# Attention times V in a fused transformer block: the third and fourth block of a chunk next to each other

## The chip, the cores and the metric

The kernel runs on one core of a Trainium2 chip. The metric is device time in microseconds (us). PE stands for TensorE (matmuls), PEld for its weight loads, DVE for VectorE, ACT for ScalarE, POOL for GpSimd and SP for SyncE, which here only issues DMAs.

## What is computed

S = 2048 rows of D = 576, H = 32 heads of 18, a hidden width F = 4608, and a causal window of 256 keys, all in bf16:

```
xn = layernorm(x)
q, k, v = split(xn @ wqkv)                       # 32 heads, Dh = 18
p = softmax(where(0 <= i - j < 256, q @ k.T * Dh**-0.5, -1e9))
h = silu(xn @ w1) * (xn @ w3)
out = x + (p @ v) @ wo + h @ w2
```

## The kernel before

The rows are taken in four chunks of 512 (`c` = 0 to 3). A chunk has three stretches on the PE, and the PE's order is written out by hand: the program lists every operation once, in one order, and each engine does its own share of the list in that order. Waits are worked out from the buffers that an operation reads and writes (`_Prog.resolve`).

- **Projections** (`proj_part`, L490): q, k and v of the chunk. q and k go through `stage` and are repacked into `qv` and `kv` by DMAs on SP and ACT (`span_main`, `span_last`, L555).
- **First half of the MLP, the units** (`unit_pairs`, L726): 36 units, each of 128 hidden features; a unit is nine pairs of matmuls of 512 columns, on two tiles of 64 rows by 128 columns of the PE. A unit takes one of three pairs of PSUM banks in turn (`job`). Then `unit_tanh` (ACT, L735) and `unit_h` (DVE, L741 and L744) make `hT[u]`. Between the pairs stand the **score steps**: `scores` (PE, L610) into a fixed pair of banks, `exps` (ACT, L619) into a slot, `masks` (POOL, L646). A chunk has 32 (chunk 0) or 40 score steps, eight groups `g` of four heads.
- **Second half of the MLP** (`p2_list`, `p2_item`, L797): the sum over 36 tiles of `hT` times w2, for each half of the output's columns (half 0, then half 1); at the end of each half the output projection `wo` of the attention's result `oT`, the residual (L828) and the output DMA. 16 items, 32 matmuls of 288 columns, make a w2 tile's worth. In half 0 the first rows of `wo` need the packs of blocks 0 to 2, and its later rows those of block 3.

**Attention times V** is done in four blocks a chunk (`pv(c, j, banks)`, L667), block j for the groups 2j and 2j + 1. A block is 72 (chunk 0) or 96 matmuls on eight tiles of 64 rows by 32 columns, of which 20 columns are used. After a block come `pv_out` (DVE transposes of two PSUM banks, L676), `o_scale` (a DVE reciprocal, L681, and a POOL product, L682), `o_turn` (DVE transposes, L689) and `o_pack` (four DMAs on SP, L714) into `oT`. Blocks 0, 1 and 2 stand between units, each when its scores are at least `PV_AFTER` = 20 matmul pairs old by the planner's `clock`; each takes a bank pair from `job` and counts `PV_COST` = 6.6 pairs, and the score steps are spread over what remains. Block 3 stands in the second half after item 8, in the banks of unit 34.

**Slots.** The result of a score step lies in a slot until its block has read it: ten buffers `pt`, four pairs of `stage` tiles (chunks 1 to 3), and for the first four steps of a chunk the last eight tiles of `hT`, which the units write later.

**Weights.** w1 and w3 come in nine tiles a chunk, each in six DMAs on SP (`load_part`, L320), into three buffers `w13`. Behind units 3, 7, ... up to 27 six parts are owed, issued one by one behind pairs of the next units; six more are issued in the second half at items 170 to 295, each behind a PE instruction. The tiles of w2 (`load_w2`, L352, ACT's queue, some on SP) are asked for six tiles ahead; in the second half four of their eight buffers lie in `w13[1]`. On SP also stand, in program order, the transposing DMA of the next chunk's last rows (L446, item 40), loads of x (items 100 and 120) and the swapped copy of xn for the next chunk (L453, item 300).

Of the kernel before, what the change touches and what calls it, by code (L numbers as in the profile page):

```python
# [5 lines left out]
dt = mybir.dt  # L6
ACT = mybir.ActivationFunctionType
ALU = mybir.AluOpType
# [156 lines left out]
def bass_parallel_sum__sliding_block__glu_gated_swiglu__prompt_kernel(  # L165
# [32 lines left out]
    with ExitStack() as es:  # L198
# [3 lines left out]

        NXP, NOF, NPT, NW13, NW2, NOD, AHEAD = 7, 4, 10, 3, 4, 2, 6
        KB, NB, NV = 64, CH // 64, 12
        ident = sb("ident", [128, 128])
        xp = [sb(f"xp{i}", [128, D]) for i in range(NXP)]
        xn = [sb(f"xn{i}", [128, 640]) for i in range(2)]
# [25 lines left out]
        def pt_slot(sl):  # L233
            kind, n = sl
            if kind == "pt":
                return pt[:, n, :, :]
            if kind == "sh":
                two = stage[:, 2 * n:2 * n + 2, :]
            else:
                two = hT[:, NF - 8 + 2 * n:NF - 6 + 2 * n, :]  # L240
            return two.rearrange("p t c -> p (t c)").rearrange("p (q r) -> p q r", r=2)

        def pt_keys(sl):
            kind, n = sl
            if kind == "pt":
                return [("pt", n)]
            if kind == "sh":
                return [("sh", 2 * n), ("sh", 2 * n + 1)]
            return [("h", NF - 8 + 2 * n), ("h", NF - 7 + 2 * n)]

        def st_keys(*tiles):
            return [("sh", t) for t in tiles]

        uq = sb("uq", [128, CH], dt.float32)
        rden = sb("rden", [128, CH // 32], dt.float32)
        oq = sb("oq", [128, CH])
        od = [sb(f"od{i}", [128, 2, CH]) for i in range(NOD)]
        oT = sb("oT", [128, 5, CH])
# [289 lines left out]
        def span_issue(a, b, moves, first, only=slice(None)):  # L548
            seen = set()
            for n, (kind, eng, tset, dst, src) in enumerate(moves):  # L550
                if n not in range(len(moves))[only]:
                    seen.add(kind)
                    continue
                keys = [(kind, g) for g in range(a, b)]
                add(eng, lambda e, dst=dst, src=src: e.dma_start(dst, src), r=st_keys(*tset), dma=f"{kind}_{a}",  # L555
                    **{"j" if kind in seen or not first else "w": keys})
                seen.add(kind)

# [45 lines left out]
        def scores(c, g, s):  # L604
            col = 0
            for n, (kb, q0, nb) in enumerate(steps_of(c)[s]):
# [6 lines left out]
                        r=[("kp" if kb < 0 else "k", g), ("q", g)], **{"j" if n else "w": [("ps", SC[r])]})  # L613
                col += nb

        def exps(c, g, s, sl):
            pt_of[(c, g, s)] = sl
            w = KB * sum(nb for _, _, nb in steps_of(c)[s])
            add("act", lambda e: e.activation(  # L619
                pt_slot(sl)[:, 0:w, :], PS[:, SC[0]:SC[1] + 1, 0:w].rearrange("p r q -> p q r"), ACT.Exp, scale=scale),  # L620
                r=[("ps", b) for b in SC], w=pt_keys(sl))

        def masks(c, g, s):

# [24 lines left out]
        def pv(c, j, banks):  # L649

            seen = set()
            n_all = sum(len(st) for st in steps_of(c))
            n = 0
            for s, st in enumerate(steps_of(c)):
                col = 0
                for kb, q0, nb in st:
                    n += 1
                    pos = (c * NB + kb) % NV
                    for gi in range(2):
                        g = 2 * j + gi  # L660
                        sl = pt_of[(c, g, s)]
                        for pr in range(2):
                            for p in range(2):
                                first = (p, gi, pr) not in seen
                                seen.add((p, gi, pr))
                                q = 2 * gi + pr
                                add("pe", lambda e, p=p, q=q, pr=pr, sl=sl, g=g, pos=pos, q0=q0, nb=nb, col=col, first=first, n=n: e.matmul(  # L667
                                    PS[32 * q:32 * q + VW, banks[p], q0 * KB:(q0 + nb) * KB],
                                    va[64 * p:64 * p + 64, pos, g, pr, :],
                                    pt_slot(sl)[64 * p:64 * p + 64, col * KB:(col + nb) * KB, pr],  # L670
                                    start=first, stop=(n == n_all), tile_position=(64 * p, 32 * q), skip_group_check=True),
                                    r=pt_keys(sl) + [("va", pos)], **{"j" if any(k[0] == p for k in seen - {(p, gi, pr)}) or not first else "w": [("ps", banks[p])]})
                    col += nb

        def pv_out(b, i):
            add("dve", lambda e: e.transpose(uqs[i], PS[:, b, :]), r=[("ps", b)], w=uq_keys[i])  # L676

        def o_scale(i):
            u3 = uqs[i].rearrange("p (n d) -> p n d", d=32)
            o3 = oq[:, :].rearrange("p (n d) -> p n d", d=32)[:, :, 0:Dh]  # L680
            add("dve", lambda e: e.reciprocal(rden[:], u3[:, :, Dh]), r=uq_keys[i], w=["rden"])  # L681
            add("pool", lambda e: e.tensor_tensor(  # L682
                o3, u3[:, :, 0:Dh], rden[:].unsqueeze(2).to_broadcast([128, CH // 32, Dh]), ALU.mult),
                r=uq_keys[i] + ["rden", "oq0"], w=["oq"])

        def o_turn(g, half):
            i = g // 2 % NOD
# [310 lines left out]
        for c in range(NC):  # L998
# [5 lines left out]
            loads = {8: (2,), 17: (3,)} if c + 1 < NC else {}  # L1004
            if c == 0:
                loads = {11: (0,), 13: (1,), 15: (2,), 17: (3,)}
            total = 9 * NF + len(att) + 3 * PV_COST
            if c:
                total += 9 * sum(COST[kind] for kind, _ in PROJ)
            start = 60 if c == 0 else 46  # L1010
# [3 lines left out]
            done = 0  # L1014
            pv_ready = {}
            free = [("pt", n) for n in range(NPT)]
            if c:
                free += [("sh", n) for n in range(4)]
            early = [("h", n) for n in range(4)]
            side = {}  # L1020
            jobs = {}
            next_pv = 0
# [4 lines left out]
            def take(n):  # L1027
                if n < len(early):
                    return early[n]
                return free.pop(0)  # L1030

            def score_step():
                nonlocal done
                g, s = att[done]
                scores(c, g, s)
                sl = take(done)
                exps(c, g, s, sl)
                masks(c, g, s)
                done += 1
                if done % (2 * NS) == 0:  # L1040
                    pv_ready[done // (2 * NS) - 1] = clock + PV_AFTER

            def spaced_step():
                nonlocal nxt, soon, clock
                score_step()
                soon = clock + 7.5
                room = last - clock - PV_COST * (3 - next_pv) - 5 * sum(v > at_u for v in xt)
                nxt = max(soon, clock + room / max(1, len(att) - done))
                clock += 1

# [18 lines left out]
            for u in range(NF):  # L1069
# [13 lines left out]
                    if n in (3, 8):  # L1083
                        owe_part(op)
                unit_tanh(u, b0[0])
                if u % 4 == 3 and u < NF - 8 and (c or u != 15):
                    owed += 6
                if next_pv in pv_ready and clock >= pv_ready[next_pv] and next_pv < 3:
# [5 lines left out]
                    for g in (2 * j, 2 * j + 1):  # L1094
                        for s in range(NS):
                            if pt_of[(c, g, s)][0] != "h":
                                free.append(pt_of[(c, g, s)])
                    later(u, lambda b=banks: (pv_out(b[0], 0), pv_out(b[1], 1), o_scale(0)))
                    later(u + 1, lambda j=j: (o_turn(2 * j, 0), o_turn(2 * j, 1), o_scale(1)))
# [40 lines left out]
            assert done == len(att) and next_pv == 3, (done, next_pv)  # L1140
# [9 lines left out]
            for item in p2_list(c):  # L1150
# [31 lines left out]
        with nc.Block() as block:  # L1182
# [29 lines left out]
```

## Time and profile before

| what | us |
|---|---|
| median of 3 runs (lowest, highest) | 558.04 (557.98, 558.10) |
| span of the profiled execution | 556.1 |
| median less span | 1.94 |
| PE in units (L726), busy, by the four tile groups of the page and its views | 182.3 + 155.3 + 5.4 + 4.7 |
| PE in the second half (L797): w2, wo | 143.9 + 20.5 |
| PE in projections (L490) | 39.0 + 22.1 |
| PE in scores (L610) | 53.8 + 19.8 |
| PE in attention times V (L667): 1068 + 216 + 156 matmuls | 20.5 + 7.8 + 4.3 |
| DVE in one unit (L741, L744), mean of one | 0.681, 0.687 |
| ACT in one exponential (L619), mean of one | 1.010 |
| w1/w3 part, w2 tile: issue to landing, median over the run | 4.3, 3.5 |

The profile is of one execution; for it the profile lists the span, from the first to the last instruction, and the timed runs are beside it with what lies around the span. Busy times of the PE overlap where tiles work side by side, so they don't add up to the span; the chain of waits in order of time gives each line's share without overlap. Starts are measured and the ends of matmuls are modelled, so a loss on the PE is read from starts. An "x4" behind a form counts instructions, and eight tiles working side by side are eight instructions. The page's "idle before" leaves out gaps below 150 ns.

### The profile page before, as it was taken

The numbers are of one execution on the slowest core, as the hardware profiler recorded it, in microseconds if no ns is written. First come the engines' busy times: TensorE is split into PE (matmuls) and PEld (weight loads), VectorE is DVE, ScalarE is ACT, GpSimd is POOL, SyncE is SP. The second block draws the span as 40 slices with busy tenths as digits, with TensorE's granted clock in tenths as the row PEclk, the third lists the DMA queues.
The fourth block names the chain that finished last, engine by engine and source line by source line (L and its number), as shares of the span: only waits on it lengthen the run. The fifth ranks groups of instructions, "written<-read, shape, count | busy, mean of one in ns | idle before, by whom it ended". The sixth has DMA issues, their size and how long they took to land.

```text
span 556.1 us, 18239 instructions
## 1 busy us (share of the span) xinstructions
PE 552.4 (99%) x8022; PEld 348.8 (63%) x8022; DVE 310.8 (56%) x587; ACT 257.6 (46%) x365; POOL 160.0 (29%) x380
## 2 busy tenths in 40 slices
PE   8999999999999999999999999999999999999998
PEld 4555445677687455477767645547777654555776
DVE  7466798610456778851056668884105567767211
ACT  7456776100286767600047776650005676666000
POOL 5323454300034445330003344533000333433000
PEclk9999999999999999999999999999999999999999
DMA  9997899677566556656856746566683684650650
GB/s 255 203 197 161 201 215 182 171 179 191 139 139 149 135 147 151 155 148 176 205 109 137 171 110 170 126 163 164 158 205 83 138 174 124 151 135 21 174 152 22
DMA packets 128038, 86.00 MB, mean 155 GB/s; under 512 B 35702, under 2 KB 125646, under 8 KB 127958
## 3 DMA queue, kind: packets, MB, share of 16 engines
q1 hardware_dynamic: 89138, 62.80, 49.7%
q10 hardware_dynamic: 38820, 22.02, 16.0%
q8 instruction: 63, 1.03, 0.8%
q14 instruction: 17, 0.14, 0.1%
HBM read 71.29 MB, written 2.36 MB: 132 GB/s over the span
## 4 chain that ended last, share of the span: by engine, by line
PE 98%; DMA 1%; ACT 0%; DVE 0%; issue 0%
PE ps L726 51%; PE ps L797 29%; PE ps L490 10%; PE ps L610 6%; PE ps L667 4%; DMA xp<-in_A_x_dram 1%; DVE stats L386 0%; ACT hT L380 0%; PE ps L419 0%; ACT sd L359 0%; ACT xnT L432 0%; DVE ofin L819 0%; DVE mv L389 0%
## 5 line engine op out<-in xcount | busy, mean ns | idle before, releaser
L726 PE MATMUL ps<-xnT,w 64*128 64x512 bf16 x1400 | 182.3, 376 | 0.0
L726 PE MATMUL ps<-xnS,w 64*128 64x512 bf16 x1120 | 155.3, 376 | 0.0
L797 PE MATMUL ps<-w,hT 64*128 64x288 bf16 x2292 | 143.9, 282 | 0.0
L741 DVE SCALAR_TENSOR_TENSOR gs<-th,ps 128x512 bf16<-128x512 bf16 x144 | 98.0, 681 | 80.1 <-ACT th L735 79.1
L619 ACT ACTIVATE pt<-ps 128x1024 bf16<-128x1024 f32 (+1 forms) x112 | 113.2, 1010 | 63.8 <-PE ps L610 62.5
L797 PEld LDWEIGHTS ps<-w,hT 64*128 64x128 bf16 x2292 | 112.0, 94 | 29.4 <-issue 0.4
L726 PEld LDWEIGHTS ps<-xnT,w 64*128 64x128 bf16 x1400 | 73.8, 94 | 55.0
L646 POOL TENSOR_TENSOR pt<-pt,mk 128x128 int32<-128x128 int32 (+1 forms) x199 | 80.3, 426 | 79.5 <-ACT pt L619 79.5
L744 DVE SCALAR_TENSOR_TENSOR hT<-gs,ps 128x512 bf16<-128x512 bf16 x144 | 98.9, 687 | 5.0
L735 ACT ACTIVATE th<-ps 128x512 bf16<-128x512 f32 x144 | 85.4, 593 | 22.2 <-PE ps L726 21.9
L726 PEld LDWEIGHTS ps<-xnS,w 64*128 64x128 bf16 x1120 | 60.1, 94 | 50.1
L503 ACT ACTIVATE stage<-ps 128x512 bf16<-128x512 f32 x16 | 9.6, 597 | 142.8 <-PE ps L490 140.5
L828 DVE TENSOR_TENSOR ofin<-ps,xp 128x288 bf16<-128x288 f32 x31 | 12.2, 451 | 110.3 <-PE ps L797 110.3
L646 POOL TENSOR_TENSOR hT<-hT,mk 128x128 int32<-128x128 int32 (+1 forms) x31 | 12.4, 420 | 170.5 <-ACT hT L619 170.5
L610 PE MATMUL ps<-qv,kv 64*128 64x320 bf16 (+4 forms) x528 | 53.8, 260 | 0.0
L610 PEld LDWEIGHTS ps<-qv,kv 64*128 64x128 bf16 x528 | 28.5, 94 | 24.7 <-issue 0.3
L490 PE MATMUL ps<-xnT,wp 64*128 64x512 bf16 (+1 forms) x360 | 39.0, 355 | 0.0
L619 ACT ACTIVATE stage<-ps 128x1024 bf16<-128x1024 f32 x24 | 24.6, 1024 | 12.6 <-PE ps L610 12.6
L689 DVE STREAM_TRANSPOSE od<-oq 128x256 bf16<-128x256 bf16 x64 | 25.8, 428 | 6.3 <-POOL oq L682 6.3
L490 PEld LDWEIGHTS ps<-xnT,wp 64*128 64x128 bf16 x360 | 20.6, 94 | 12.6 <-ACT va L539 0.4
L490 PE MATMUL ps<-wv,xnT 64*128 64x288 bf16 x288 | 22.1, 284 | 0.2 <-ACT xnT L432 0.2
L646 POOL TENSOR_TENSOR stage<-stage,mk 128x128 int32<-128x128 int32 (+1 forms) x42 | 16.9, 421 | 17.4 <-ACT stage L619 17.3
(73 smaller groups left out, 337.6 us busy)
## 6 DMA issues: line engine op xcount, KB each, us to landing
w<-in_B_w_dram SPq DMA_DIRECT2D x210, 192.0 KB, 4.3
w<-in_B_w_dram ACTq DMA_DIRECT2D x70, 288.0 KB, 3.5
xp<-in_A_x_dram SPq DMA_DIRECT2D x29, 144.0 KB, 3.3
out_dram<-ofin SPq DMA_DIRECT2D x31, 72.0 KB, 3.2
xnS<-xnT SPq DMA_DIRECT2D x8, 256.0 KB, 5.2
oT<-od SPq DMA_DIRECT2D x56, 36.0 KB
pt<-in_A_wqkv_dram SPq DMA_DIRECT2D x4, 288.0 KB, 5.0
hT<-in_B_w_dram SPq DMA_DIRECT2D x6, 192.0 KB, 6.3
```

What stands on the lines that cost most here:

```text
L490: op = add("pe", lambda e, out_=out_, st=st, mv=mv, n=n, r0=r0, first=first: e.matmul(out_, st, mv, start=first, stop=(part == 1 and n == ...
L610: add("pe", lambda e, r0=r0, out_=out_, kb=kb, q0=q0, nb=nb: e.matmul(out_, kb4[r0:r0 + 64, g, kb + NV - NB, :] if kb < 0 else kv[r0:r0 + ...
L619: add("act", lambda e: e.activation(pt_slot(sl)[:, 0:w, :], PS[:, SC[0]:SC[1] + 1, 0:w].rearrange("p r q -> p q r"), ACT.Exp, scale=scale) ...
L646: add("pool", lambda e, vb=vb, mm=mm: e.tensor_tensor(vb, vb, mm, ALU.mult), r=(key if n == 0 else []) + ["mk"], **{"w" if n == 0 else "j" ...
L667: add("pe", lambda e, p=p, q=q, pr=pr, sl=sl, g=g, pos=pos, q0=q0, nb=nb, col=col, first=first, n=n: e.matmul(PS[32 * q:32 * q + VW, banks ...
L689: add("dve", lambda e: e.transpose(od[i][:, g % 2, c0:c0 + CH // 2], oq[:, c0:c0 + CH // 2]), r=["oq", "oq0"], **{"j" if half or g % 2 els ...
L726: op = add("pe", lambda e, n=n, r0=r0, r=r, k=k, src=src: e.matmul(PS[:, b0 + r, :], wt[r0:r0 + 64, k, fl * 128:(fl + 1) * 128], src, star ...
L735: add("act", lambda e: e.activation(th[i][:], PS[:, bg, :], ACT.Tanh, scale=0.5), r=[("ps", bg)], w=[("th", i)])
L741: add("dve", lambda e: e.scalar_tensor_tensor(out=gs[i][:], in0=th[i][:], scalar=1.0, in1=PS[:, bg, :], op0=ALU.add, op1=ALU.mult), r=[("t ...
L744: add("dve", lambda e: e.scalar_tensor_tensor(out=hT[:, u, :], in0=gs[i][:], scalar=0.5, in1=PS[:, bu, :], op0=ALU.mult, op1=ALU.mult), r= ...
L797: op = add("pe", lambda e: e.matmul(PS[:, bank, 0:w], stat, move, start=new, stop=False, skip_group_check=True, **tile), r=keys, after=hel ...
L828: add("dve", lambda e: e.tensor_tensor(ofin[:, o, :], PS[:, bank, 0:HD], xp[xs[n]][:, d0:d0 + HD], ALU.add), r=[("ps", bank), ("xp", xs[n] ...
```

## The change

Block 2 leaves the units. Blocks 2 and 3 stand together in the second half after item 24, block 2 in the banks of unit 34 and block 3 in those of unit 35. Their `pv_out` and reciprocals come first, for all four banks; then product, turns and packs, group by group. Two of the four transposed results go into `pt` slots that the blocks have read (`borrow`), and `rden` has four copies.

Since the scores of two blocks have to be kept until then, there are more slots: up to 16 tiles of `hT` for the first eight steps of chunks 1 to 3, the `stage` pairs in chunk 0 too, and at the end of the units eight slots in the w1/w3 buffers 2 and 0 (`wx`), from unit 28 and unit 32 on. So the next chunk's w1/w3 tile is no longer loaded behind unit 27; the second half issues twelve parts, from item 90 on every 18 items. The late moves of a key span get a semaphore of their own. The planner counts two blocks in place of three.

```diff
+        NHP = 8
+        WX = [(2, i) for i in range(4)] + [(0, i) for i in range(4)]
...
+            if kind == "wx":
+                b, i = WX[n]
+                flat = w13[b][:, :, :].rearrange("p a b -> p (a b)")
+                return flat[:, 2 * CH * i:2 * CH * (i + 1)].rearrange("p (q r) -> p q r", r=2)
...
-                two = hT[:, NF - 8 + 2 * n:NF - 6 + 2 * n, :]
+                two = hT[:, NF - 2 * NHP + 2 * n:NF - 2 * NHP + 2 + 2 * n, :]
...
-        rden = sb("rden", [128, CH // 32], dt.float32)
+        rden = [sb(f"rden{i}", [128, CH // 32], dt.float32) for i in range(4)]
...
-                add(eng, lambda e, dst=dst, src=src: e.dma_start(dst, src), r=st_keys(*tset), dma=f"{kind}_{a}",
+                add(eng, lambda e, dst=dst, src=src: e.dma_start(dst, src), r=st_keys(*tset), dma=f"{kind}_{a}" if first else f"{kind}r_{a}",
...
+        def lent_keys(c, sl):
+            keys = pt_keys(sl)
+            if sl[0] != "wx":
+                return {"w": keys}
+            b = WX[sl[1]][0]
+            if (c, b) in lent_w13:
+                return {"w": keys, "j": [("w13", b)]}
+            lent_w13.add((c, b))
+            return {"w": keys + [("w13", b)]}
...
-                r=[("ps", b) for b in SC], w=pt_keys(sl))
+                r=[("ps", b) for b in SC], **lent_keys(c, sl))
...
+        def borrow(slots):
+
+            for i, n in enumerate(slots):
+                uqs[2 + i:3 + i] = [pt[:, n, :, :].rearrange("p q r -> p (q r)").bitcast(dt.float32)]
+                uq_keys[2 + i:3 + i] = [[("pt", n)]]
...
-            total = 9 * NF + len(att) + 3 * PV_COST
+            total = 9 * NF + len(att) + 2 * PV_COST
...
-            if c:
-                free += [("sh", n) for n in range(4)]
-            early = [("h", n) for n in range(4)]
+            free += [("sh", n) for n in range(4)]
+            early = [("h", n) for n in range(4 if c == 0 else 0, NHP)]
+            late = [("wx", n) for n in range(len(WX))]
...
-                room = last - clock - PV_COST * (3 - next_pv) - 5 * sum(v > at_u for v in xt)
+                room = last - clock - PV_COST * (2 - next_pv) - 5 * sum(v > at_u for v in xt)
...
-                if u % 4 == 3 and u < NF - 8 and (c or u != 15):
+                if u % 4 == 3 and u < NF - 12 and (c or u != 15):
                     owed += 6
...
                 elif n == 8:
                     load_w2(c, AHEAD - 1, after=(last_pe(),))
-                    banks = jobs[NF - 2]
-                    pv(c, 3, banks)
-                    pv_out(banks[0], 0)
-                    pv_out(banks[1], 1)
-                    o_scale(0)
-                    o_turn(6, 0)
-                    o_turn(6, 1)
-                    o_scale(1)
-                    o_turn(7, 0)
-                    o_turn(7, 1)
-                    o_pack(3, "sp")
+                elif n == 24:
+                    pairs = (jobs[NF - 2], jobs[NF - 1])
+                    borrow([m for kind, m in (pt_of[(c, g, s)] for g in range(4, G) for s in range(NS)) if kind == "pt"][:2])
+                    for j in range(2):
+                        pv(c, 2 + j, pairs[j])
+                    for i in range(4):
+                        pv_out(pairs[i // 2][i % 2], i)
+                        o_recip(i)
+                    for g in range(4):
+                        o_scale(g)
+                        o_turn(4 + g, 0)
+                        o_turn(4 + g, 1)
+                        if g % 2:
+                            o_pack(2 + g // 2, "sp")
...
-                elif n in (170, 195, 220, 245, 270, 295) and c + 1 < NC:
+                elif n in range(90, 300, 18) and c + 1 < NC:
                     load_part((last_pe(),))
```

More of the change, by code (lines that the diff above doesn't have):

```diff
@@ L244, in pt_keys @@
             kind, n = sl
-            if kind == "pt":
-                return [("pt", n)]
+            if kind in ("pt", "wx"):
+                return [(kind, n)]
             if kind == "sh":
                 return [("sh", 2 * n), ("sh", 2 * n + 1)]
-            return [("h", NF - 8 + 2 * n), ("h", NF - 7 + 2 * n)]
+            t = NF - 2 * NHP + 2 * n
+            return [("h", t), ("h", t + 1)]
         def st_keys(*tiles):
@@ L614, in scores @@
                 col += nb
+        lent_w13 = set()
+        def lent_keys(c, sl):
[7 more added lines that the diff above has]
+            return {"w": keys + [("w13", b)]}
         def exps(c, g, s, sl):
@@ L671, in pv, with o_recip @@
                                     start=first, stop=(n == n_all), tile_position=(64 * p, 32 * q), skip_group_check=True),
-                                    r=pt_keys(sl) + [("va", pos)], **{"j" if any(k[0] == p for k in seen - {(p, gi, pr)}) or not first else "w": [("ps", banks[p])]})
+                                    r=pt_keys(sl) + [("va", pos)] + ([("w13", WX[sl[1]][0])] if sl[0] == "wx" else []), **{"j" if any(k[0] == p for k in seen - {(p, gi, pr)}) or not first else "w": [("ps", banks[p])]})
                     col += nb
+        def borrow(slots):
+            for i, n in enumerate(slots):
+                uqs[2 + i:3 + i] = [pt[:, n, :, :].rearrange("p q r -> p (q r)").bitcast(dt.float32)]
+                uq_keys[2 + i:3 + i] = [[("pt", n)]]
         def pv_out(b, i):
-            add("dve", lambda e: e.transpose(uqs[i], PS[:, b, :]), r=[("ps", b)], w=uq_keys[i])
+            to = uqs[i]
+            add("dve", lambda e: e.transpose(to, PS[:, b, :]), r=[("ps", b)], w=uq_keys[i])
+        def o_recip(i):
+            u3 = uqs[i].rearrange("p (n d) -> p n d", d=32)
+            add("dve", lambda e: e.reciprocal(rden[i][:], u3[:, :, Dh]), r=uq_keys[i], w=[("rden", i)])
         def o_scale(i):
@@ L680, in o_scale @@
             o3 = oq[:, :].rearrange("p (n d) -> p n d", d=32)[:, :, 0:Dh]
-            add("dve", lambda e: e.reciprocal(rden[:], u3[:, :, Dh]), r=uq_keys[i], w=["rden"])
             add("pool", lambda e: e.tensor_tensor(
-                o3, u3[:, :, 0:Dh], rden[:].unsqueeze(2).to_broadcast([128, CH // 32, Dh]), ALU.mult),
-                r=uq_keys[i] + ["rden", "oq0"], w=["oq"])
+                o3, u3[:, :, 0:Dh], rden[i][:].unsqueeze(2).to_broadcast([128, CH // 32, Dh]), ALU.mult),
+                r=uq_keys[i] + [("rden", i), "oq0"], w=["oq"])
         def o_turn(g, half):
@@ L1029, in take @@
                     return early[n]
-                return free.pop(0)
+                if free:
+                    return free.pop(0)
+                sl = late.pop(0)
+                assert at_u >= (28 if sl[1] < 4 else 32), (c, n, at_u)
+                return sl
             def score_step():
@@ L1035, in score_step @@
                 scores(c, g, s)
-                sl = take(done)
-                exps(c, g, s, sl)
+                exps(c, g, s, take(done))
                 masks(c, g, s)
                 done += 1
-                if done % (2 * NS) == 0:
+                if done % (2 * NS) == 0 and done <= 4 * NS:
                     pv_ready[done // (2 * NS) - 1] = clock + PV_AFTER
@@ L1085, in bass_parallel_sum__sliding_block__glu_gated_swiglu__prompt_kernel @@
                 unit_tanh(u, b0[0])
-                if u % 4 == 3 and u < NF - 8 and (c or u != 15):
+                if u % 4 == 3 and u < NF - 12 and (c or u != 15):
                     owed += 6
-                if next_pv in pv_ready and clock >= pv_ready[next_pv] and next_pv < 3:
+                if next_pv in pv_ready and clock >= pv_ready[next_pv]:
                     j = next_pv
@@ L1093, in bass_parallel_sum__sliding_block__glu_gated_swiglu__prompt_kernel @@
                     clock += PV_COST
[L1094 to L1099, printed above, removed]
+                    was = [pt_of[(c, g, s)] for g in (2 * j, 2 * j + 1) for s in range(NS)]
+                    assert all(NF - 2 * NHP + 2 * n > u for kind, n in was if kind == "h"), (c, u)
+                    free += [sl for sl in was if sl[0] != "h"]
+                    later(u, lambda b=banks: (pv_out(b[0], 0), o_recip(0), pv_out(b[1], 1), o_scale(0)))
+                    later(u + 1, lambda j=j: (o_turn(2 * j, 0), o_turn(2 * j, 1), o_recip(1), o_scale(1)))
                     later(u + 2, lambda j=j: o_turn(2 * j + 1, 0))
@@ L1139, in bass_parallel_sum__sliding_block__glu_gated_swiglu__prompt_kernel @@
                     xs = [load_x(c * TB + tt) for tt in range(TB)]
-            assert done == len(att) and next_pv == 3, (done, next_pv)
+            assert done == len(att) and next_pv == 2, (done, next_pv)
             ACC[:] = [[*JOBS[job_ctr % 3], *SC], [*jobs[NF - 2], *jobs[NF - 1]]]
```

## The prediction

> **What bounds the kernel now.** I read the page first, then the list of what the PE waited for, then the chain of waits in order of time around one block of attention times V, then the timeline of the same stretch. The page:
>
> ```profile
> PE 552.4 (99%) x8022; PEld 348.8 (63%) x8022; DVE 310.8 (56%) x587; ACT 257.6 (46%) x365; POOL 160.0 (29%) x380
> PEclk9999999999999999999999999999999999999999
> PE 98%; DMA 1%; ACT 0%; DVE 0%; issue 0%
> ```
>
> The PE is busy for 552.4 of 556.1 us, at the full granted clock throughout, and it is 98% of the chain that ended last. A busy PE can still hide short losses, so the second view is what it waited for in the whole run (us in total, times, longest):
>
> ```profile
> PE ps L867 <- DVE oq L862: 1.2, 1, 1.2
> PE ps L490 <- ACT xnT L432: 0.2, 1, 0.2
> ```
>
> Both waits lie at the start of the program. So nothing that the change takes from DVE, ACT, POOL or a queue can gain time: a gain has to be time within the PE's own stream, and any loss has to be a new wait of the PE. The chain of waits in order of time (start, us, line, matmuls) shows what a block costs in that stream; first chunk 1 (the block j = 2 in the units, then the block j = 3 in the second half), then j = 2 of chunk 0:
>
> ```profile
> 214.65 0.65 PE ps L726 x6
> 215.30 1.32 PE ps L667 x96
> 216.62 0.33 PE ps L610 x6
> ...
> 218.67 0.22 PE ps L610 x6
> 218.89 1.94 PE ps L726 x18
> ...
> 239.25 1.30 PE ps L667 x89
> ```
>
> ```profile
> 84.97 0.98 PE ps L667 x65
> 85.95 0.30 PE ps L610 x4
> ...
> 87.98 0.19 PE ps L610 x4
> ```
>
> A unit is 18 matmuls, nine pairs, in 1.94 us: 0.216 us for a pair of 512 columns. A block of chunk 1 passes 2560 columns through each of its eight tiles (96 matmuls over 8 tiles; steps of 320, 192, 320, 192, 320, 128, 64, 320, 128, 64, 256 and 256 columns), at that rate 1.08 us. The chain gives it 1.32, and the score step behind it takes 0.33 where an ordinary one of six matmuls takes 0.22. The block costs 1.43 us, 0.35 over its columns. In chunk 0 it is 1920 columns, 0.81 us, against 0.98 + 0.30 - 0.19 = 1.09: 0.28 over. The reader is to see that a block has a surcharge that its columns don't explain; the question is how much of it sits at the ends.
>
> **The change, part by part.** The timeline of the same block (start, us, engine, line, form) splits the surcharge:
>
> ```profile
> 214.92 0.38 PE L726 MATMUL ps<-xnT,w 64*128 64x512 bf16 x2
> 215.23 1.00 PE L667 MATMUL ps<-pt,va 64*20 64x320 bf16 x60
> ...
> 216.27 0.29 PE L667 MATMUL ps<-pt,va 64*20 64x256 bf16 x4
> 216.30 0.32 PE L667 MATMUL ps<-stage,va 64*20 64x256 bf16 x4
> 216.55 0.31 PE L610 MATMUL ps<-qv,kv 64*128 64x320 bf16 x2
> 216.70 0.25 PE L610 MATMUL ps<-qv,kb 64*128 64x128 bf16 x4
> ```
>
> Into the block: the last pair of the unit starts at 214.92 and the first tile of the block at 215.23, 0.31 where a pair takes 0.216: 0.09 lost as the tiles change from 64*128 to 64*20. Within: 215.23 to 216.27 is 1.04 for the first eleven steps, 2304 columns or 0.97: 0.07 lost, spread over the steps. Out: 216.27 to 216.55 is 0.28 for the last step of 256 columns (0.108): 0.17 lost, of which some 0.07 is that the eight tiles of the last step start one behind another (216.27, 216.30 and later) and 0.10 the change back to 64*128. Behind it: the first pair of scores takes 0.15 where 320 columns are 0.135: 0.01. Together 0.34, the 0.35 of the chain.
>
> *The join.* Block 2 leaves the units and stands ahead of block 3, with the same tiles. One change in and one change out of the 64*20 tiles go, 0.09 + 0.10 + 0.01 = 0.20. The stagger of 0.07: each tile goes its own way, so a stagger at the end of block 2 is carried through block 3 and paid once at its end; I take 0.05 of it as saved (block 3 starts with 0.02 of its own). No trace of before shows two blocks in a row, so the ends are 0.19 (nothing of the stagger) and 0.27 (all of it); I take 0.25 for chunks 1 to 3, nearest to the tiles' own starts. In chunk 0, 0.28 less nine steps at 0.07/11 each is 0.22; I take 0.21. Sum: 0.21 + 3 x 0.25 = 0.96 us, with ends of 0.76 and 1.03.
>
> *The work that moves with block 2* (two transposes of L676, two reciprocals of L681, two products of L682 on POOL, four turns of L689, four pack DMAs of L714) costs nothing if it ends before the output projection reads it. The stretch after block 3 in chunk 1, from the timelines of DVE, POOL and SP, then that of the PE:
>
> ```profile
> 240.73 0.70 DVE L676 STREAM_TRANSPOSE uq<-ps 128x512 f32<-128x512 f32 x1
> 241.37 0.67 DVE L676 STREAM_TRANSPOSE ofin<-ps 128x512 f32<-128x512 f32 x1
> 241.97 0.20 DVE L681 RECIPROCAL rden<-uq 128x16 f32<-128x16 f32 x1
> 242.96 0.77 DVE L689 STREAM_TRANSPOSE od<-oq 128x256 bf16<-128x256 bf16 x2 [0.79 <-POOL oq L682]
> ```
>
> ```profile
> 238.26 2.85 POOL L590 COPY kb<-kv 128x256 f32<-128x256 f32 x8
> ```
>
> ```profile
> 245.45 3.00 SPq L714 DMA_DIRECT2D oT<-od  x4
> 248.49 1.22 SPq L446 DMA_TRANSPOSE xnT<-xn  x1
> ```
>
> ```profile
> 257.03 2.12 PE L797 MATMUL ps<-wo,oT 64*128 64x288 bf16 x32
> 258.99 2.25 PE L797 MATMUL ps<-w,hT 64*128 64x288 bf16 x34
> ```
>
> ```profile
> out_dram<-ofin SPq DMA_DIRECT2D x8, 72.0 KB, 3.8
> ```
>
> On this stretch's clock the blocks start 16 items later than block 3 does now. 32 matmuls (16 items) take 258.99 - 257.03 = 1.96, so the first starts at 239.25 + 1.96 = 241.2, and they end at 242.5 and 243.7 (1.30 and 1.2). POOL has copied its keys by then (238.26 + 2.85). Four transposes and reciprocals, at most 0.70 + 0.20 each, end at 246.1. The first turns follow at once, 0.77; three rounds of a POOL product (0.79 of DVE idle) and turns (0.77) end at 251.6. The second four packs are issued 0.75 apart, the last at 253.9. No row gives a pack's landing; the nearest is the last one above, an output of 72 KB beside crowded transfers, 3.8 us from issue: 257.7. The projection's rows that need this block come after half of the 1.96 us, at 257.03 + 0.98 + 1.2 (the block now ahead of them) = 259.2: 1.5 us to spare. The first four packs land near 255, for 258.2.
>
> *Queues.* On SP the transfer of L446 now stands behind eight packs and starts near 254.5 in place of 248.5; its data is read by the next chunk's projections. Twelve w1/w3 parts follow where there were six (the load at unit 27 is dropped). Each waits on a PE item, 18 items apart, and what is queued behind them (outputs, the swap of xn) waits on later items anyway. ACT's queue keeps its order.
>
> *Buffers.* The exponentials go into more of hT, into stage and into two w1/w3 tiles. Each such write waits on a reader that stands ahead of its own scores on the PE, or on a repack of keys that chunk 0 has read for its scores by then: no new wait, taken at nothing. Without that cover the next scores wait as long as the exponential is late. The separate semaphore of the late key spans adds a wait instruction per span: nothing, beside pairs of 0.216 us. Block 3 now uses the banks of the last unit, whose last DVE step is this row:
>
> ```profile
> L744 DVE SCALAR_TENSOR_TENSOR hT<-gs,ps 128x512 bf16<-128x512 bf16 x144 | 98.9, 687 | 5.0
> ```
>
> The PE gets there 27 items and a block after that unit, 27 x 0.122 + 1.3 = 4.6 us, against some five such steps on DVE: hidden.
>
> **The rivals.**
>
> *Crowded transfers, slower.* The six parts added to the second half are 1.15 MB on engines that are already loaded there. The transfers of chunk 1 from 237.5 to 258 us, then from 258 to 281 (x, KB each, median us to landing):
>
> ```profile
> w<-in_B_w_dram ACTq DMA_DIRECT2D x11, 288.0 KB, 3.4
> ```
>
> ```profile
> DMA packets 6053, 4.27 MB, mean 186 GB/s; under 512 B 302, under 2 KB 5939, under 8 KB 6050
> ...
> w<-in_B_w_dram ACTq DMA_DIRECT2D x7, 288.0 KB, 6.0
> w<-in_B_w_dram SPq DMA_DIRECT2D x6, 192.0 KB, 5.4
> ```
>
> A w2 tile is asked for five tiles ahead, 5 x 1.96 = 9.8 us, and takes 6.0 when the w1/w3 parts run beside it, 3.4 when they don't. For it: 6.0 against 3.4. Against it: the new parts start in the quieter window, and 3.8 us are spare. At 186 GB/s, the later window's mean, 1.15 MB are 6.2 us; were a w2 tile late by all of it, the PE would wait 6.0 + 6.2 - 9.8 = 2.4 us in each of three chunks, 558.04 - 0.96 + 7.2 = 564.3; it decides from 9.8 us on. The Trainium skill (Trainium Kernel Development and Optimization, Key Constraints) speaks against the change here: transfers issued from SP and ACT share the same 16 engines and interleave. By that rule alone the 3.8 us would be overdrawn; this trace agrees on the sharing (3.4 against 6.0).
>
> *The packs land late, slower.* 1.5 us are spare, so the PE waits at the projection once a pack takes over 5.3 us. At the 6.0 us of the w2 tiles it would be 0.7 us in each of four chunks: 558.04 - 0.96 + 2.8 = 559.9. For it: the bounds above. Against it: a pack is 36 KB where a w2 tile is 288, and the packs stand ahead of all new parts on their queue.
>
> *The whole surcharge goes.* If the steps' own 0.07 and the stagger are also start-up that a running stream does not pay: 0.28 + 3 x 0.35 = 1.33, 556.7. Against it: the 0.07 is spread over steps in mid-block. The Trainium skill (TensorE: Matmul & The Clock Gate, Single matmul latency) gives a lone warm matmul about 166 ns more than its columns; at two bared ends a block in four chunks that would be an estimate of 1.33 us as well. The 0.09 at the entry disagrees with it here.
>
> *It doesn't do what it says.* If the loss is tied to entering each block (other weights, other banks) and not to the change of tiles, or small new waits eat it: 558.0. For it: no row shows two blocks in a row. Against it: steps in mid-block change weights and banks too, and together lose 0.07.
>
> **How the numbers follow.** The profiled execution's own span of 556.1 less 0.96 is 555.1; the runs' median lies 558.04 - 556.1 = 1.94 above the span: 557.1. Chances: the forecast 0.62 (556.9 to 557.3, the ends of the sum with the runs' scatter of 0.1), the whole surcharge 0.08, no gain 0.10, crowded transfers 0.11, late packs 0.09. A measurement of this kernel can tell about 0.2% (1.1 us) from no change, and the forecast of -0.17% lies inside that. Faster by more needs 556.9 or less: 0.08, and 0.05 from the forecast's lower edge, 0.13. Slower by more: the two waits, 0.20. Within: 0.67. The range leaves out the two waits: 556.7 (the whole surcharge) to 558.6 (no gain and a wait of half a microsecond).
>
> **What would show it.** Right: four rows of L667 fewer in the chain, one of about 2.5 us in each second half (2.2 in chunk 0), ordinary score steps where block 2 stood, the PE's list of waits as short as now. Within a joined block, some 0.01 and not 0.2 between the halves. Wrong: a PE wait at L797 on a w2 transfer or an oT pack; an L610 group that waits for an exponential; a joined block that takes the sum of two.

## The result: slower by 0.6%

The changed kernel takes 561.05 us (median of 6 runs, 560.34 to 564.56) where the kernel before takes 558.04 (6 runs, 557.89 to 558.10): the ratio is 1.0063 [1.0046, 1.0081]. The prediction, 557.1 with a range up to 558.6, was wrong. The profiled execution of after took 560.34 us with a span of 558.6, 2.5 more than the span before.

The page of after, the rows that answer to those of before, and the row of the queue that brings instructions (packets, MB, share):

```profile
PE 552.6 (99%) x8022; PEld 354.3 (63%) x8022; DVE 314.6 (56%) x587; ACT 257.6 (46%) x365; POOL 160.7 (29%) x380
PEclk9999999999999999999999999999999999999999
q8 instruction: 63, 1.03, 0.8%
PE 99%; issue 0%; DVE 0%; ACT 0%
```

The PE has the same number of matmuls and the full clock, and 0.2 us more of busy time. So the 2.5 us are idle time of the PE. What it waited for, on the PE and then, in the other view, on its weight loads:

```profile
PE ps L826 <- issue: 2.2, 4, 0.9
PE ps L896 <- DVE oq L891: 1.2, 1, 1.2
PE ps L497 <- ACT xnT L439: 0.2, 1, 0.2
```

```profile
PEld ps L826 <- DMA w<-in_B_w_dram: 0.7, 2, 0.3
```

The first row is new. The PE stood still four times in the second half, once in each chunk, and the releaser is "issue": nothing that the profile shows held it up. The w2 row is new as well, both waits in chunk 1; from the starts of the matmuls they cost the PE 0.4 us. The chain of waits in order of time of chunk 1 shows the place:

```profile
237.91 2.69 PE ps L826 x44
240.60 2.46 PE ps L686 x163
243.06 1.33 PE ps L826 x19
244.39 0.52 issue
244.90 2.13 PE ps L826 x31
```

The joined block takes 2.46 us, as the prediction said it would (2.5). Then 19 ordinary matmuls pass, and the PE stops. These 19 matmuls are worth 19 x 0.061 = 1.16 us (32 took 1.96) and stand in 1.33 + 0.52 = 1.85: 0.69 lost. Worked out in this way from single starts, the four waits are 1.08, 0.68, 0.54 and 0.58 us: 2.9 in all.

**What the waits have in common.** The program of the PE comes to it by DMA, in 63 packets of 16 KB. 63 x 256 = 16128, and the PE has 8022 matmuls, 8022 weight loads and some 90 instructions more in the records, so a packet holds 256 instructions. Matmuls from the start up to each wait (the windows view, x counts; as many weight loads stand beside them):

```profile
0.00:106.50 106.50, 104.52 (x1365) 1.00 0.83 188
0.00:244.50 244.50, 242.02 (x3402) 1.00 0.72 168
0.00:382.70 382.70, 379.76 (x5439) 1.00 0.70 162
0.00:520.50 520.50, 517.16 (x7475) 1.00 0.68 157
```

From wait to wait it is 2037 matmuls, 2037 weight loads and, in the records, 22 other instructions: 4096, sixteen packets (the last count is one short: its window cuts a pair). The waits are at the seams of packets. The next packet had just come. In the view of the DMAs, its transfer begins between 242.5 and 242.7, and in 243.4 to 246.1, the time of the wait, no packet of that queue begins; only data moves:

```profile
q8 instruction: 1, 0.02, 33.0%
```

```profile
q10 hardware_dynamic: 309, 0.18, 24.9%
```

From the records of single packets and starts (us):

| chunk | first instruction of a packet | the next one's transfer begins | ends | its first instruction | PE lost |
|---|---|---|---|---|---|
| 0 | 103.35 | 104.63 | 105.62 | 106.89 | 1.08 |
| 1 | 241.48 | 242.56 | 243.61 | 244.90 | 0.68 |
| 2 | 379.69 | 380.74 | 381.66 | 383.08 | 0.54 |
| 3 | 517.34 | 518.18 | 519.61 | 520.90 | 0.58 |

The next packet is on its way only 0.84 to 1.28 us after the first instruction of the one before it, travels for 0.92 to 1.43, and its first instruction runs 1.27 to 1.42 after it has come: 3.4 to 3.6 us. The PE was through with its 256 instructions in 2.3 to 2.9, since a joined block is 384 instructions (288 in chunk 0) in 2.46 us (1.85). In the kernel before, the same seams in chunks 1 to 3 were crossed 1.7 to 2.3 us after the packet had come, by single records as above: no wait, and some 0.3 to 0.4 us to spare at the least.

The first theory, then, is **instruction supply**: the block saves what it should, but it uses up a packet of instructions faster than the next one comes. The rivals: something that the change moved (slots, lent banks and weight buffers, loads) holds the PE up; or the data transfers do, w2 above all. The expectations call supply A and the rivals without it B and C; times in them are counted from 0.31 us after the start of the span.

### The profile page after: what moved, and what is told of

It reads as the page before. It is cut to its first block, busy times and chain, and to the rows that moved or that the text cites. A ratio compares the mean times of both kernels' runs of the same rounds, so it can differ in the third digit from the quotient of the medians.

```text
span 558.6 us, 18252 instructions
## 1 busy us (share of the span) xinstructions
PE 552.6 (99%) x8022; PEld 354.3 (63%) x8022; DVE 314.6 (56%) x587; ACT 257.6 (46%) x365; POOL 160.7 (29%) x380
## 4 chain that ended last, share of the span: by engine, by line
PE 99%; issue 0%; DVE 0%; ACT 0%
PE ps L755 50%; PE ps L826 29%; PE ps L497 10%; PE ps L617 6%; PE ps L686 3%; PE ps L896 1%; PE ps L426 0%; ACT xnT L439 0%; DVE ofin L848 0%; DVE oq L891 0%
## 5 line engine op out<-in xcount | busy, mean ns | idle before, releaser
L755 PE MATMUL ps<-xnS,w 64*128 64x512 bf16 x1120 | 157.8, 376 | 0.0
L826 PEld LDWEIGHTS ps<-w,hT 64*128 64x128 bf16 x2292 | 115.7, 94 | 29.2 <-issue 3.7
L638 ACT ACTIVATE pt<-ps 128x1024 bf16<-128x1024 f32 (+1 forms) x80 | 80.9, 1011 | 44.9 <-PE ps L617 44.9
L665 POOL TENSOR_TENSOR pt<-pt,mk 128x128 int32<-128x128 int32 (+1 forms) x143 | 57.7, 426 | 49.8 <-ACT pt L638 49.4
L665 POOL TENSOR_TENSOR hT<-hT,mk 128x128 int32<-128x128 int32 (+1 forms) x52 | 20.8, 420 | 174.1 <-ACT hT L638 174.1
L638 ACT ACTIVATE hT<-ps 128x1024 bf16<-128x1024 f32 (+1 forms) x28 | 28.4, 1015 | 10.0 <-PE ps L617 9.9
L638 ACT ACTIVATE stage<-ps 128x1024 bf16<-128x1024 f32 (+1 forms) x24 | 24.4, 1015 | 11.1 <-PE ps L617 10.2
L638 ACT ACTIVATE w<-ps 128x1024 bf16<-128x1024 f32 (+1 forms) x20 | 20.3, 1013 | 10.8 <-PE ps L617 10.7
```

Source lines behind the costliest of these rows:

```text
L638: add("act", lambda e: e.activation(pt_slot(sl)[:, 0:w, :], PS[:, SC[0]:SC[1] + 1, 0:w].rearrange("p r q -> p q r"), ACT.Exp, scale=scale) ...
L665: add("pool", lambda e, vb=vb, mm=mm: e.tensor_tensor(vb, vb, mm, ALU.mult), r=(key if n == 0 else []) + ["mk"], **{"w" if n == 0 else "j" ...
L755: op = add("pe", lambda e, n=n, r0=r0, r=r, k=k, src=src: e.matmul(PS[:, b0 + r, :], wt[r0:r0 + 64, k, fl * 128:(fl + 1) * 128], src, star ...
L826: op = add("pe", lambda e: e.matmul(PS[:, bank, 0:w], stat, move, start=new, stop=False, skip_group_check=True, **tile), r=keys, after=hel ...
```

## The experiments

**Both blocks in the second half, but apart.** Block 2 alone at item 8, block 3 alone at item 38, each with its own transposes, product, turns and packs. The two `pt` slots that the change lends to the transposes (`borrow`) aren't needed here; all else is as after.

```diff
                 elif n == 8:
                     load_w2(c, AHEAD - 1, after=(last_pe(),))
-                elif n == 24:
-                    pairs = (jobs[NF - 2], jobs[NF - 1])
...
+                    banks = jobs[NF - 2]
+                    pv(c, 2, banks)
...
+                elif n == 38:
+                    banks = jobs[NF - 1]
+                    pv(c, 3, banks)
...
```

> The changed kernel with the two blocks in the second half parted: block 2 after item 8, block 3 after item 38, each with its own transposes, product, turns and packs behind it. Slots, lent buffers, w1/w3 parts and the planner stay as changed. Theory A (supply of instructions): 30 items, 120 instructions and 3.7 us stand between the blocks, no packet of 256 is used up in under 3.5 us, no wait: the kernel before plus nothing, 557.9 to 558.4 us. Theory C (the moved transfers and lent buffers cost the time): still 561.

It took 557.93 against 557.94, ratio 1.0 [0.9991, 1.0009], and has no new wait. The moved work, the slots, the lent w1/w3 buffers and the twelve parts cost nothing. That rival has fallen: it takes the joining. (The lent `pt` slots are tested by the runs at items 10 and 11, which keep them.)

**The joined block at other items.** Only the item in `elif n == 24:` differs: 11, 10, 34.

> The changed kernel with the joined blocks after item 11 of the second half in place of item 24. Theory A: the same place against the packets as with 200 more instructions ahead (packet boundaries 218 to 230 instructions into the joined blocks of chunks 1 to 3, 116 in chunk 0): the waits go, 557.1 to 557.6 us. Theory B: the waits stay behind the joined blocks, 561. Theory C: the packs land 1.6 us earlier, which helps nothing that waits now, 561.

> The joined blocks after item 10, one item earlier than the version that beat the kernel before. Theory A: in chunk 0, where at item 11 the next packet's first instruction came 1.29 us after the end of its transfer, the least seen, the small wait of about 0.1 us goes; elsewhere 1.5 to 2.0 us were there and stay above 1.3: 557.0 to 557.4 us beside 557.3 at item 11. If the banks of unit 35 are then late (read by DVE until about 2.4 us into the second half), block 3 waits up to 0.1 us instead.

> The changed kernel with the joined blocks after item 34, ten items later. Theory A: the packets' ends stand 382 to 394 instructions into the joined blocks of chunks 1 to 3 and 280 into that of chunk 0, so a packet goes nearly whole within a block: waits of about 1.6 us in chunks 1 to 3 and 1.2 us in chunk 0 in place of 0.6 and 1.1, the first instruction behind each wait 1.2 to 1.5 us after the end of a packet's transfer: 564 us. Theory B (two blocks in a row as such): 561. Theory C: the packs land 1.2 us later, still ahead of the projection: 561.

Item 11 took 557.29 against 557.91, ratio 0.9989 [0.9980, 0.9998]; item 10 557.22 against 557.94, 0.9986 [0.9977, 0.9995]; item 34 564.55, 1.0122 [1.0108, 1.0136]. The same work in the same order differs by 7 us with the place. The chain of chunk 1 at item 11, then at item 34:

```profile
236.55 1.72 PE ps L826 x28
238.27 2.48 PE ps L686 x156
240.75 5.25 PE ps L826 x84
```

```profile
241.92 2.45 PE ps L686 x167
244.37 1.98 issue
246.35 0.28 PE ps L686
```

At item 34 the block itself stops in chunks 0 and 1, at a seam that lies within it, and in chunks 2 and 3 the PE stops just behind the block (it lost some 1.2, 2.2, 2.0 and 1.7 us in the four chunks, and 0.3 at a later seam). At item 11 the PE goes on without a stop in chunks 1 to 3; in chunk 0 it loses 0.1 us. In chunks 1 to 3 its packet began as the units ended, and the next one's transfer had begun 0.6 to 0.9 us *before* the packet's first instruction: 256 instructions then passed in 2.4 to 2.7 us and nothing waited. So it isn't a fixed least time for a packet; it is how early the transfer of the next one begins.

**The packets shifted against the work.** The warm-up ahead of the program (`warm`) gets more and smaller matmuls, so every later instruction moves within its packet.

```diff
-        warm(4, [CH] * 9)
+        warm(4, [42] * 109)
```

```diff
-        warm(4, [CH] * 9)
+        warm(4, [CH // 4] * 36)
```

> The changed kernel, with nothing moved: only the nine warm-up matmuls of 512 columns at the start are cut into 109 of 42 columns (4578 columns in place of 4608). That puts 200 more instructions ahead of everything. Theory A (supply of instructions): the PE's instructions arrive in packets of 256; the four waits behind the joined blocks all stand at the first instruction of a packet, and a joined block uses up a packet faster than the next one comes. A new packet then begins some 222 to 234 instructions into the joined blocks of chunks 1 to 3 and some 120 into that of chunk 0, so that no 320 instructions in a row pass in less than about 4.1 us: the waits go, 557.1 to 557.6 us. Theory B (the wait belongs to the two blocks in a row, to their banks or the lent buffers): nothing changes, 561. Theory C (crowded transfers): nothing changes, 561.

> The changed kernel with the nine warm-up matmuls cut into 36 of 128 columns: 54 more instructions ahead of everything, the same columns. Theory A: a packet now ends 368 to 380 instructions into the joined blocks of chunks 1 to 3, so that it is used up in about 2 us, and the waits there grow from 0.55 to 0.7 us to about 1.7 us each; in chunk 0 the wait shrinks from 1.1 to about 0.6 us. In all about 2.8 us more than the changed kernel, 563.8 us. Theories B and C: nothing changes, 561.

The second came out as A had it: 565.85, ratio 1.0140 [1.0126, 1.0154], with the waits now inside the blocks:

```profile
PE ps L686 <- issue: 6.7, 4, 1.9
```

The first was a miss: 563.2, ratio 1.0093 [1.0078, 1.0108]. The waits did move to the new seams, 223 instructions and more into the blocks of chunks 1 to 3, but they didn't go:

```profile
PE ps L686 <- issue: 2.7, 3, 1.1
...
PE ps L497 <- POOL wp L936: 0.8, 1, 0.8
PE ps L826 <- DMA w<-in_B_w_dram: 0.7, 2, 0.4
PE ps L617 <- ACT stage L638: 0.5, 1, 0.5
```

The transfer that mattered began 0.5 to 1.1 us after the first instruction of the packet ahead; I had taken it to begin as early as at item 11. A shift by instructions places the waits, but their size can't be had from the position in the packet alone. Of the other rows, the first is the start-up, which the longer warm-up put back by 0.8 us; besides, the PE waited twice for w2, and one score step for an exponential.

**One block of the kernel before doubled.** Nothing of the change is in it; the matmuls of block 3 are issued twice, into the same banks.

```diff
                     pv(c, 3, banks)
+                    pv(c, 3, banks)
```

> The kernel before the change, with the matmuls of block 3 issued twice in a row into the same banks (the second pass writes the same sums): a joined block without more slots, without lent buffers, without more w1/w3 parts in the second half and without block 2 moved. The added matmuls cost 0.84 us in chunk 0 and 1.16 in the others, 4.3 in all. Theory A: the packets' ends now stand 241 instructions into the doubled block of chunk 0, 410 of chunk 1, 227 of chunk 2 and 300 of chunk 3; waits of about 0, 1.0, 0 and 1.1 us, in chunk 3 within the block: 564.4 us. Theory B, banks and lent buffers, and theory C: no wait at all, 562.3 us; theory B, two blocks in a row as such: a wait of about the same size in every chunk.

It took 568.87, ratio 1.0196 [1.0182, 1.0210], and waits in exactly the two chunks that A named:

```profile
PE ps L667 <- issue: 2.2, 1, 2.2
PE ps L797 <- issue: 1.6, 1, 1.6
```

They are larger than expected (1.8 and 2.2 from the starts, not 1.0 and 1.1), the second copies cost 4.3, and some 1.8 more is the clock, in 510 to 530 us (granted clock in the column behind the count):

```profile
510.00:530.00 20.00, 17.82 (x372) 0.91 0.23 56
```

By the clock's records it was granted at half for 3.4 us, from 1.0 us after the longer wait had ended. All four runs of this kernel have a mean clock of 0.997 where the profiled runs of the other kernels have 1.0. Whether the wait brings the drop about isn't shown: the shift by 54 instructions has waits nearly as long (2.1 us by the starts), and its profiled run kept the full clock.

**One block alone, wholly within a packet.** The kernel before, block 3 at item 18 and not 8.

```diff
                 elif n == 8:
                     load_w2(c, AHEAD - 1, after=(last_pe(),))
+                elif n == 18:
                     banks = jobs[NF - 2]
                     pv(c, 3, banks)
```

> The kernel before with one edit: block 3 alone stands at item 18 instead of item 8, so no block is joined to another. By the counts its 192 instructions then begin 2 to 20 instructions after the start of a packet of 256 in chunks 1 to 3. Instruction supply: a single block takes 1.39 us where a joined one takes 2.45, so the packet lasts only 1 us less than one without a block; the earlier packets of this kernel with a block in them had some 0.4 us to spare, so the next packet comes 0 to 0.4 us late in chunks 1 to 3: 558.0 to 559.2. The joining itself as the cause (two blocks in one group, their lent banks, one after the other): no block is joined here, no wait, 557.9 to 558.2.

557.96 against 557.96, ratio 1.0 [0.9991, 1.0009]: no wait, at the good end of what supply expected and no worse than the rival, so this run tells little apart. The packets with the block lasted 3.3, 3.5 and 3.7 us, and the next ones had come 1.7 to 2.1 us before they were needed.

**Is the packet late because data stands ahead of it?** In after, the engines are loaded with w2 until just before the packet's transfer begins, which looks like a queue. Three kernels: after with the two w2 loads ahead of it put behind the block; after with one of them issued twice; and item 10 with the two loads put behind.

```diff
-                if sl + AHEAD < 2 * NFC:
+                if sl == 0:
+                    pass
+                elif sl + AHEAD < 2 * NFC:
...
-                elif n == 8:
-                    load_w2(c, AHEAD - 1, after=(last_pe(),))
+                elif n in (30, 34):
+                    load_w2(c, AHEAD - 1 + (n == 34), after=(last_pe(),))
```

> The kernel after the change with two w2 loads of each chunk issued later: the one at item 8 at item 30, the one behind the first w2 tile (item 15) at item 34, both behind the joined block, so that no data is asked for in the 1 to 2 us before the PE's late instruction packet. In the kernel after, the transfers were busy from about 240.4 to 242.2 us, and the instruction packet's own transfer began at 242.25, as they went quiet. If the instruction packet is late because it stands behind the w2 data on the transfer engines: its transfer begins about 0.4 us or more earlier, the waits of 0.5 to 1.1 us shrink to 0 to 0.4, and the w2 waits of chunk 1 go or stay: 557.2 to 559.6. If it is late only because the PE runs through 256 instructions faster than the next packet can be asked for (1.05 to 1.18 us from a packet's first instruction to the next transfer even where the engines are idle): the waits stay, 560.3 to 561.3.

> The kernel after the change with one w2 load of each chunk issued twice, at items 8 and 12 (the same tile, the same data), 288 KB or about 0.9 us of transfers more in front of the late instruction packet. Behind the data on the engines: the packet's transfer begins up to 0.9 us later and each of the four waits grows by up to that: 562 to 564.7. Asked for too late only: the waits stay, and the w2 waits of chunk 1 (0.4 us) grow a little: 560.5 to 562.

> The kernel after the change with the joined block at item 10, where it made 557.22, and the two w2 loads at items 30 and 34 as in the run above. Behind the data: the packet waits of 0.16 (chunk 0) and 0.18 us (chunk 1) that were left at item 10 go, 556.7 to 557.2. Asked for too late only: 557.2 as before.

Quiet engines changed nothing at item 24: 560.9, ratio 1.0045 [1.0031, 1.0059]. The windows from the packet's first instruction to the next one's transfer, in the four chunks (us; the last columns are clock, DMA share, GB/s), and what the PE waited for:

```profile
103.42:104.04 0.62, 0.62 (x75) 1.00 0.14 26
242.70:244.30 1.60, 1.60 (x138) 1.00 0.00 0
381.01:382.07 1.06, 1.06 (x110) 1.00 0.00 0
520.21:521.05 0.84, 0.84 (x80) 1.00 0.00 0
```

```profile
PE ps L826 <- issue: 2.4, 4, 1.0
PE ps L826 <- DMA w<-in_B_w_dram: 1.5, 3, 0.8
```

In chunks 1 to 3 the engines stood idle, in chunk 0 nearly so, and the transfer still began 0.62 to 1.60 us after the packet did. The waits at the seams behind the blocks sum to 2.9 us from the starts, as before, and w2 tiles now come late as well. (The first row's four waits are not these four: the view leaves out that of chunk 3 and counts a later seam. The profiled run, 562.91, is the slowest of the five.) The load issued twice took 561.7, 1.0063 [1.0050, 1.0075], within what "asked for too late" expected, and the transfers began 0.8 to 1.4 us after the packet's first instruction. So the data isn't what makes the packet late at item 24. At item 10 it had a share: with the loads put behind, the transfers of chunks 0 and 1 began 0.84 and 0.94 us after the packet in place of 1.81 and 1.80, the small waits that were left there (0.16 and 0.18) went, and the kernel took 556.98, ratio 0.9986 [0.9977, 0.9994]. Whether that is faster than item 10's 557.22 the intervals don't tell. Both beat the kernel before and after.

Crowded engines can delay a packet elsewhere, though. In these two runs at item 24 a seam among ordinary w2 matmuls of chunk 0, at 130.7 us, cost the PE 0.45 and 0.50 us: there the w1/w3 parts ran beside w2, and the packet's transfer began 5.5 and 5.8 us after the first instruction of the packet ahead. In after such transfers began up to 5.1 us late, just in time; in the second half of the kernel before it was 2.8 at the most.

## Why the prediction was wrong

**The bound was right.** The PE is still the whole chain, and only its own stream could gain.

**The sum of the join was right.** From the pair ahead of each block to the instruction behind it, the two blocks together against the joined one saved 0.23, 0.26, 0.26 and 0.17 us: 0.92, where the sum said 0.96. Its parts (the two changes of tiles, the stagger) were not measured one by one. The joined block of 2.2 us that was expected in chunk 0 doesn't follow from the prediction's own row, since two blocks apart are 2 x 0.98 there; it took 1.85. Where nothing waits, the whole forecast comes out: 556.98 against 557.93 is -0.95. The rival in which the whole surcharge goes (1.33) did not occur, and neither did the one in which the join saves nothing.

**The moved work and the buffers were right.** The blocks apart are as fast as before, and in after no projection waits on a pack and no score step on an exponential.

**The step that failed** comes behind the sentence that any loss "has to be a new wait of the PE". That sentence held; what failed is the search for such waits, which went through engines, queues, buffers and data and so put all else at nothing. It took for granted that the PE's next instruction is always there, and the sum 558.04 - 0.96 has no term for it. The list of waits before had no such row, and that was read as "no such limit", when it was a margin of some 0.4 us. The rival in which small new waits eat the gain stopped at no change, 558.0, and the range at a wait of half a microsecond. The block saved 0.92, and the supply of instructions took 2.9 back, w2 0.4: +2.4 of the 2.5 us of span. The profile of before could have warned: the page has the row of the instruction queue, and a joined block passes 384 instructions in the time in which the second half elsewhere passes some 80 (32.7 in a us, two for each of 32 matmuls in 1.96).

**Crowded transfers** were a rival at 2.4 us a chunk; late w2 tiles cost 0.4 in all, in chunk 1. **Late packs** did not occur.

The Trainium skill (Runtime: NRT & Kernel Launch, Instruction fetch mechanics) describes refills in blocks of 16 KiB, 256 instructions, and calls the crossing mostly hidden, since the sequencer issues more slowly than the refill. The trace agrees on the blocks, and disagrees on the second point for this stretch: 2.9 us in four crossings.

**What stays open** is what sets the moment at which a packet's transfer begins. At the joined blocks of chunks 1 to 3, in the runs at items 10 to 34, it came 0.1 to 1.1 us ahead of the previous packet's first instruction where units stood before that, and 0.7 to 1.8 behind it where the second half or a block did. That a lead counted in instructions is worth less time where instructions are short would fit, and was not tried by itself. Several kernels with such waits also scatter at the full clock, by 3.5 us with the w2 loads put behind, where those without stay within 1.5; why, the single traces don't show. Of the runs of after five lie within 0.8 us; the sixth, 564.56, had a mean clock of 0.997, which is worth some 1.7 us of its distance.

## What to carry to other kernels

Before many small matmuls are packed side by side, count instructions as well as columns: here 256 instructions came in a packet, and where the PE waited for the next one beside a joined block, the packet with its wait took 2.8 to 4.2 us. A stretch that ran through a packet faster got by only where the next transfer had begun early. An "issue" wait with the counts of instructions between such waits a multiple of 256 points to that limit, and then the place of the burst in the stream decides: the same block gained 0.1% right behind the slow units and lost 0.6 to 1.2% when it stood 13 or 23 items (1.6 or 2.8 us) later.

## What the runs showed of the hardware

- A packet of 256 PE instructions mostly took 0.9 to 1.4 us of transfer, and where the PE waited for it, its first instruction ran 1.15 to 1.6 us after the transfer's end.
- With the transfer engines idle, the next packet's transfer still began 0.8 to 1.6 us after the PE had entered the packet ahead, in the joined blocks of chunks 1 to 3 at item 24 with the w2 loads put behind. With w1/w3 parts and w2 under way, it began up to 5.8 us after (one load issued twice).
- In the profiled run with the doubled block the granted clock averaged 0.91 over 510 to 530 us, 20 x 0.09 = 1.8 us, behind a wait of the PE of 2.2 us.
